# A transformer block in split fp32: engines chosen when the instruction list is made, other buffers for late norms and three X blocks, two x tiles by ScalarE's queue

## The chip, the cores and the metric

The kernel runs on one core of a Trainium2 chip. The metric is the time of one execution on the device in microseconds (us), the median of several runs. The core has five engines that run their own instruction lists beside each other: TensorE (PE; its weight loads are shown as PEld), VectorE (DVE), ScalarE (ACT), GpSimd (POOL) and SyncE (SP), which here issues nearly all DMAs. A matmul writes one of 8 PSUM banks of 128 x 512 fp32; only VectorE and ScalarE read them.

## The reference

One block: `h = x + A(layernorm(x))`, `h2 = h + B(layernorm(h))`, x of 2048 tokens by 448, all in fp32.

```python
def A(x):          # sliding-window attention, 16 heads of 28, window 256
    q, k, v = split(x @ wqkv)
    scores = q @ k.T * 28 ** -0.5, kept where 0 <= i - j < 256
    return (softmax(scores) @ v) @ wo
def B(x):          # gated GELU, 448 -> 1792 -> 448
    return (gelu_tanh(x @ w_gate) * (x @ w_up)) @ w_down
```

## The kernel before, in words

**Precision.** TensorE multiplies a rounded fp32 form (`F32R`). So each operand is split into a high part (`to_hi`, a copy on ScalarE) and a low part (`to_lo`, source minus high part, on VectorE or GpSimd), and a product is the sum of high x high, high x low and low x high.

**How the order is made.** Nothing is issued directly. Every operation is put on a list by `op(engine, cost, latency, key, fn, reads, writes, bank, port, ...)`; dependencies follow from the names that it reads and writes. `Lists.run` then plays the list through on the host with a simple clock: at each step each engine has candidates whose dependencies are met, and among those that could start within a few hundredths of a microsecond of the earliest the one with the lowest `key` is taken. The order that comes out is the order of the instructions on each engine; on the chip the engines only wait for each other. `port=True` marks operations of VectorE and GpSimd that the clock lets not overlap. `allowed` says which banks a kind of product may use, and `idle` fills TensorE's waits in the first microseconds with transposes of the identity. Most constants at the top of the file are keys or lags for this list.

**Start.** SP's queue loads the 16 x tiles (`load`, 128 tokens by 448 each, into `hres`), the q/k weights (`wqk_load`) and the v weights (`wv_load`). The first tiles are normalised (`layer_norms`, `normalise`), transposed on TensorE (`tr`, L454) and split into xT.

**Attention.** Four chunks of 512 tokens by four groups of four heads are 16 blocks. A block loads its q and k (`loads`, L711), makes scores (L729), maxima (L733), probabilities (L802, exponentials at L806), masks them on GpSimd (L821) and multiplies them with v (`attend`, L840); `MERGE` says whether a block's `attend` is one piece or two halves. `project_tile` (L678) makes q and k of the next chunk meanwhile, `values` (L624) v, `output` (L900) the product with wo.

**Feed-forward part.** 14 passes m, each for 256 columns of gate and up and 1024 tokens. The first three (`CL`) use plain products with 512 tokens a turn (`cslot`, `cfull`, L1139); the other 11 use one level of Strassen's scheme, 7 instead of 8 products of half-size blocks, two of them side by side in the array (`both`, L1340). For it the tokens are combined: `tokens_x(cp, ...)` loads blocks of the transposed normalised tokens (`loads_x`, L1010, and `fill`, L1016), makes sums (`XADD`, L1051 to L1057) and splits them (`split`, `XLO` for the low parts). Token half 0 puts all of its X blocks into `late[0]` (xo), which opens only when attention is over; half 1 puts them into xT, at the places in `XPLACE`. `weight_set` does the same with the weights: sums at L1210, low parts at L399 by `WLO` or `WLO2`, where a table names GpSimd or VectorE for each.

A product's bank is copied away by ScalarE (`copied`, L1346) or added to a buffer by VectorE (`added`, L1350), then Gelu (L1362, in the plain passes L1164), the product of gate and up (L1368, in the plain passes L1179) and the split into high and low part. The down product (`down_half`, L1414) uses half-height tiles, in two phases that write the same four banks with the halves exchanged; before the second phase a 1x1 read of the bank, `seen` (L1260, on ScalarE), makes TensorE wait until the first is complete. `out_add` (L1431) adds the finished banks to `hres` and stores them. All of TensorE's feed-forward operations are chained in one fixed order by `queued`; the down halves are put between the other products by `pause`.

The keys of the feed-forward part start at `FFN` = 1000 and grow by 2 x `UNIT` = 200 a pass. Norms of the feed-forward part (`ln2`) for tokens 0 to 1023 are made in attention, the rest in the first passes (`norms_later`); tiles from 8 on use three parts of the then free v buffer (`VM`). A tile goes out through `turn` (L490, L493) in transposed form.

Of the kernel before, what the change touches and what calls it, by code (L numbers as in the profile page):

```python
# [28 lines left out]
MERGE = (1, 1, 1, 0, 1, 1, 1, 1, 0, 1, 1, 1)  # L29
# [5 lines left out]
VLAST = (-22, 7, 26, 34)  # L35
ELAST = 1
LAG_P = 14.5
LAG_V = 11.0
EDGE = 12
WIN = 10  # L40
FFN = 1000
FULL = 3
CL = 3
CWL = 100
LATER = 4
ALONE = 5
# [7 lines left out]
WLO2 = ('pool', 'dve', 'pool', 'dve')  # L54
XADD2 = ('pool', 'pool', 'dve', 'dve')
XLO2 = ('pool', 'pool', 'dve', 'pool', 'dve')
XLATE = 150
XSTEP = 200
XWHOLE = (0, 0)
HASTE = 300  # L60
OUTK = 40
WLATE = 190
UNIT = 100
XADD = ('dve', 'dve', 'pool', 'dve')
XLO = ('dve', 'pool', 'dve', 'dve', 'dve')
WLO = ('dve', 'pool', 'dve', 'dve')
DKEY = 368
# [30 lines left out]
class Op:  # L98
    __slots__ = ("eng", "cost", "lat", "key", "fn", "deps", "users", "left", "banks", "port", "ready", "start", "fin",
                 "size", "tag", "mode")  # L100
# [9 lines left out]
class Lists:  # L110
# [6 lines left out]
    def op(self, eng, cost, lat, key, fn, r=(), w=(), bank=None, port=False, size=0, tag=None, after=(), part=None, mode=0):  # L117
        o = Op()
        o.eng, o.cost, o.lat, o.key, o.fn, o.port, o.size, o.tag, o.mode = eng, cost, lat, key, fn, port, size, tag, mode
        o.deps, o.users, o.ready, o.start = set(after), [], 0.0, None  # L120
        o.banks = () if bank is None else tuple(bank) if type(bank) is list else (bank,)
# [33 lines left out]
    def run(self, allowed, idle):  # L155
# [10 lines left out]
        for o in self.ops:  # L166
            o.left, o.ready, o.start = len(o.deps), 0.0, None
            for b in o.banks:
                b.k, b.left = None, 0
            if not o.left:  # L170
                cand[o.eng].append(o)
# [5 lines left out]
        def start_of(e, o):  # L177
            t = max(free[e], o.ready)
            if o.port:
                t = max(t, lock["pool" if e == "dve" else "dve"] - 0.03)  # L180
# [25 lines left out]
        while n:  # L206
            best = None
            for e in E:
                c = choice(e)
                if c is not None and (best is None or c[0] < best[0]):  # L210
                    best = c
            t, o, got = best
            e = o.eng
# [5 lines left out]
            cand[e].remove(o)  # L219
# [26 lines left out]
            for u in o.users:  # L246
                u.left -= 1
                u.ready = max(u.ready, o.start + cost if e == u.eng == "pe" else o.fin + WAKE[u.eng])
                if not u.left:
                    cand[u.eng].append(u)  # L250
# [4 lines left out]
def block_kernel(ctx: ExitStack, tc, x, wqk_in, wv_in, wo_in, gu_in, rest_in, cw_in, down_in, out):  # L255
# [122 lines left out]

    def HR(t):
# [60 lines left out]
    def normalise(t, key, kind):  # L440
# [3 lines left out]
        home = [VM[2 * t % 3], VM[(2 * t + 1) % 3]] if spare else [(lambda i=i: xn[i], XN(i), None) for i in range(2)]  # L444
# [36 lines left out]
        op("act", 0.49, 0.605, key, lambda: to_hi(xT[:, 0:4, c], view()), (), [XT(tc)], b)  # L481
        op("dve", 0.89, 0.87, key, lo, [XT(tc)], [XT(tc)], b)
# [13 lines left out]
    def turned(t, key, kind):  # L496
# [5 lines left out]
            put, [span("xT", tc, 0.5)])  # L502
        dma(key + 0.1, 80, lambda: nc.sync.dma_start(f(xT[:, 3, c]), d[D - 128:D]), put,
            [span("xT", tc + 0.5, 0.5)], cost=0.55)
# [16 lines left out]
    def start():  # L521
# [5 lines left out]
        for t in range(4):  # L527
            load(t, -100 + t)
        wv_load(0, -95)
# [23 lines left out]
        op("pool", 0.1, 0.1, -101, lambda: nc.gpsimd.memset(nhalf, -0.5), (), ["nhalf"])  # L553
# [63 lines left out]
    def values(t, p, n):  # L617
# [4 lines left out]
        for a in range(NP):  # L622
# [3 lines left out]
                stop=(a == NP - 1)), [XT(col(t)), *(WV(p + i, h, wb) for i in range(n))], () if a else [V(t, p, n)], b, tag="v")  # L626
# [40 lines left out]
    def project_tile(c, m):  # L667
# [7 lines left out]
        for a in range(NP):  # L675
# [4 lines left out]
                stop=(a == NP - 1)), [span("xT", cc, 4), WQK(m, h)], (), b, tag="proj")  # L680
# [18 lines left out]
    got = {}  # L699
# [232 lines left out]
    XPLACE = {(1, 0): (0, 0), (1, 2): (3, 0), (1, 1): (0, 1), (1, 3): (3, 1), (0, 0): (0, 2), (0, 1): (3, 2),  # L932
              (0, 2): (0, 3), (0, 3): (3, 3), (1, 4): (6, 0), (0, 4): (6, 1)}
# [5 lines left out]
    VM = [(lambda i=i: v_m[:, 512 * i:512 * i + 512], span("vm", 512 * i, 512), None) for i in range(7)]  # L939
# [851 lines left out]
```

## Time and profile before

| | |
|---|---|
| median of 3 runs | 698.39 us (696.53 to 698.69) |
| the profiled execution | 698.2 us, its span 696.5 us |
| mean granted TensorE clock | 0.999 |
| DMA | 116.25 MB, mean 167 GB/s |

The span goes from the first to the last instruction; the execution's own time holds 1.7 us more. In the lines of the profile, `L1340 PE MATMUL bank<-xT,proj` is a matmul issued by line 1340 of the file, which writes `bank` and reads `xT` and `proj`; `x12` counts instructions merged into one row; `[0.77 <-ACT e L1260]` is idle time of the engine ahead of it and what ended it.

### The profile page before, as it was taken

To read this page: it belongs to the slowest core of one execution; us is meant where nothing else is said; L and a number is where in the kernel's file an instruction comes from. 1 tells how busy PE (TensorE), PEld (TensorE's weight loads), DVE (VectorE), ACT (ScalarE), POOL (GpSimd) and SP (SyncE) were. 2 spreads that over 40 slices of the span, in tenths; PEclk is the share of its full clock that TensorE was granted. 3 is DMA by queue.
4 is the path that set the end of the run, shared out by engine and by line. 5 is a ranking of instruction groups with operands and counts; after the bars stand their busy time and mean duration, and the time that the engine had idled before them with its cause. 6 is when DMAs were issued, how large, how long until landed. Compare 5 with 4: busy or idle time off the path is not lost. (4 is left out here: it accounts for less than half of the span.)

```text
span 696.5 us, 15373 instructions
## 1 busy us (share of the span) xinstructions
PE 685.1 (98%) x5544; PEld 578.1 (83%) x5544; DVE 513.4 (74%) x1213; ACT 413.9 (59%) x911; POOL 311.1 (45%) x422
## 2 busy tenths in 40 slices
PE   8999999999999999999999999999999999999997
PEld 7888888888888878878878888888888888888886
DVE  7967678987798788838775789776555756866764
ACT  7747576877768667776554565644534545546431
POOL 5612654644456446441452779634303445447000
PEclk9999999999999999999999999999999999999999
DMA  9997967688688697406767775415004744533102
GB/s 315 277 285 216 286 173 202 183 230 244 166 210 247 183 273 207 165 1 178 197 181 158 213 205 170 119 51 171 20 16 131 211 132 132 161 116 88 44 15 105
DMA packets 104691, 116.25 MB, mean 167 GB/s; under 512 B 44632, under 2 KB 82392, under 8 KB 104040
## 3 DMA queue, kind: packets, MB, share of 16 engines
q1 hardware_dynamic: 104472, 115.17, 58.0%
q8 instruction: 43, 0.70, 0.4%
q14 instruction: 32, 0.26, 0.1%
q10 hardware_dynamic: 144, 0.11, 0.0%
HBM read 84.97 MB, written 44.47 MB: 186 GB/s over the span
## 5 line engine op out<-in xcount | busy, mean ns | idle before, releaser
L733 DVE CUSTOM_DVE_ANT_0 mt<-bank,mt 128x384 bf16<-128x384 f32 (+2 forms) x256 | 126.4, 526 | 26.8 <-PE bank L729 24.8
L806 ACT ACTIVATE pp<-bank 128x384 f32<-128x384 f32 (+1 forms) x188 | 90.8, 527 | 18.5 <-PE bank L802 16.3
L678 PE MATMUL bank<-xT 128*128 128x512 f32 x308 | 96.1, 399 | 0.0
L1340 PE MATMUL bank<-xT,proj 64*128 64x512 f32 x735 | 94.7, 389 | 0.2 <-DVE v L1350 0.2
L1340 PEld LDWEIGHTS bank<-xT,proj 64*128 64x128 f32 x735 | 72.1, 184 | 13.4 <-DVE v L1350 0.8
L729 PE MATMUL bank<-rk,rq 84*128 84x384 f32 (+2 forms) x256 | 81.0, 337 | 0.0
L802 PE MATMUL bank<-rq,rk 104*128 104x384 f32 (+2 forms) x352 | 80.6, 302 | 0.0
L821 POOL TENSOR_SCALAR_AFFINE_SELECT pp<-pp 128x512 f32<-128x512 f32 x96 | 60.6, 651 | 40.2 <-ACT pp L806 38.6
L1414 PE MATMUL bank<-proj,gh 64*128 64x448 f32 x624 | 71.5, 362 | 1.2 <-ACT e L1260 1.2
L802 PEld LDWEIGHTS bank<-rq,rk 104*128 104x128 f32 x352 | 59.4, 190 | 9.3 <-ACT pp L806 1.5
L1431 DVE TENSOR_TENSOR hres<-bank,hres 128x448 f32<-128x448 f32 (+1 forms) x113 | 62.8, 611 | 5.6 <-PE bank L1414 5.6
L1414 PEld LDWEIGHTS bank<-proj,gh 64*128 64x128 f32 x624 | 59.2, 184 | 8.0 <-ACT e L1260 1.9
L678 PEld LDWEIGHTS bank<-xT 128*128 128x128 f32 x308 | 55.6, 189 | 6.8 <-DVE proj L399 0.5
L1210 POOL TENSOR_TENSOR xn<-proj 64x128 f32<-64x128 f32 (+2 forms) x36 | 33.3, 928 | 52.5 <-DMA proj<-gu 46.8
L1260 ACT ACTIVATE e<-bank 1x1 f32<-1x1 f32 x139 | 21.7, 156 | 55.9 <-PE bank L1414 41.3
L729 PEld LDWEIGHTS bank<-rk,rq 84*128 84x128 f32 x256 | 47.6, 189 | 7.0 <-DVE mx L733 1.4
L396 ACT ACTIVATE rq<-bank 8x512 fp32r<-8x512 f32 x64 | 37.7, 589 | 22.1 <-PE bank L760 21.0
L399 DVE TENSOR_TENSOR proj<-proj 128x448 fp32r<-128x448 f32 (+2 forms) x42 | 25.8, 630 | 32.0 <-ACT proj L396 27.0
L624 PE MATMUL bank<-proj,xT 128*128 128x448 f32 (+1 forms) x220 | 49.1, 334 | 0.0
L1340 PE MATMUL bank<-xo,proj 64*128 64x512 f32 x366 | 47.7, 389 | 0.1
L1340 PEld LDWEIGHTS bank<-xo,proj 64*128 64x128 f32 x366 | 36.0, 184 | 7.1 <-DVE v L1350 0.8
L1350 DVE TENSOR_TENSOR raw<-bank,raw 128x512 f32<-128x512 f32 x22 | 15.2, 691 | 35.1 <-PE bank L1340 35.0
(193 smaller groups left out, 1474.3 us busy)
## 6 DMA issues: line engine op xcount, KB each, us to landing
rk<-k SPq DMA_DIRECT2D x44, 336.0 KB
rq<-q SPq DMA_DIRECT2D x32, 336.0 KB
gu<-in_gu_dram SPq DMA_DIRECT2D x18, 480.0 KB
proj<-gu SPq DMA_DIRECT2D x24, 288.0 KB
q<-proj SPq DMA_DIRECT2D x12, 448.0 KB
proj<-down SPq DMA_DIRECT2D x22, 224.0 KB
proj<-gu SPq DMA_DIRECT2D x24, 192.0 KB
k<-proj SPq DMA_DIRECT2D x9, 448.0 KB
```

The source lines that it names most:

```text
L396: nc.scalar.activation(dst, src, AF.Copy)
L624: op("pe", mm(224 * n), 0.29 if n == 1 else 0.38, key + a / 16, lambda a=a, h=h, wb=wb, xb=xb: nc.tensor.matmul(bank[b.k][:, 0:224 * n], x ...
L678: op("pe", mm(512) + 0.002, 0.403, key, lambda a=a, h=h, wb=wb, xb=xb: nc.tensor.matmul(bank[b.k], wqk[m][:, h, wb, :], xT[:, xb, cc * 128 ...
L729: nc.tensor.matmul(bank[b.k][:, o:384], rq[u][0:3 * DH, j, i * 128:i * 128 + 128], rk[u][0:3 * DH, j, m0 * 128:(i + 3) * 128], start=True, ...
L733: nc.vector.tensor_tensor_reduce(junk[s % 2][:, o:384], bank[b.k][:, o:384], mask[:, o:384], 1.0, -BIG, OP.add, OP.max, mx[:, i, j:j + 1])
L802: nc.tensor.matmul(bank[b.k][:, n * i:n * i + n], rk[u][0:104, j + i, m * 128:m * 128 + 128], rq[u][0:104, j + i, lo * 128:(hi + 1) * 128] ...
L806: nc.scalar.activation(pp_cols(o, n)[:, j:j + G], bank[b.k][:, 0:G * n].rearrange("p (g t) -> p g t", g=G), AF.Exp, scale=SCALE)
L821: nc.gpsimd.affine_select(a, a, pattern=[[0, 4], [-cm, 128]], compare_op=op_, fill=0.0, base=0, channel_multiplier=cm)
L1210: arith("pool", w, key + 1, lambda e: e.tensor_tensor(xn_m[HALF[side], o:o + w], a(), b(), op=what), rd, [tok])
L1340: nc.tensor.matmul(bank[b.k], w, xarea(u.cp, xl, xs, side)[:, xk], start=p in (1, 2, 5) and not k and not t, stop=t == 2, tile_position=(6 ...
L1414: nc.tensor.matmul(bank[banks[q].k][:, 0:D], h[oh][0]()[HALF[x], q * 128:q * 128 + 128], d[wh][0]()[HALF[x]], start=not ph and not y and n ...
L1431: op("dve", 0.07 + w * 0.463 / D, 0.163 + w * 0.463 / D, key, lambda: nc.vector.tensor_tensor(hres[:, t, c0:c0 + w], bank[b.k][:, c0:c0 + ...
```

## The change

- An operation may carry `alts`, for each engine that could do it the cost, the latency, the function and the port mark. It is a candidate on all of them; the one on which the list's clock would end it first gets it.
- With `FLEX = 'xwsc'` this holds for the X sums and low parts (x), the weight sums and low parts (w) (GpSimd or VectorE), `seen` (s) and `copied` (c) (ScalarE or VectorE). The tables `XADD`, `XLO`, `WLO` stay as first values only.
- X blocks (1,2), (1,1) and (1,0) of token half 0 lie in xT and are loaded from key `X0LOAD` on behind block 15's loads (`X0HOLD`); the other X blocks of both halves get other places.
- Late norms use two other parts of the v buffer and a part of `raw_m` (`SPARE`), and the plain passes' gate buffers move to `VM[0:4]`.
- x tiles 2 and 3 are issued by ScalarE, around a first small activation that brings the function table's loading there. `nhalf` is set ahead of it.
- Dependencies on xT are named by half (`XTB`): the four high parts and the three low parts apart.
- Keys and lags have other values. `MERGE` makes block 15's `attend` two halves instead of block 12's.

```diff
-MERGE = (1, 1, 1, 0, 1, 1, 1, 1, 0, 1, 1, 1)
+MERGE = (1, 1, 1, 0, 1, 1, 1, 1, 1, 1, 1, 0)
-VLAST = (-22, 7, 26, 34)
-ELAST = 1
+VLAST = (-10, 3, 26, 30)
+ELAST = 0
-LAG_V = 11.0
+LAG_V = 12.0
-WIN = 10
+WIN = 8
+FLEX = 'xwsc'
-CWL = 100
+CWL = 75
-CKEY = (220, 242)
-CWKEY = (236, 240, 190, 306)
-EARLY = (15, 16, 15, 15)
-CHOLD = (10, 13, 11, 13)
-X0KEY = 1060
-XTIME = (10, 6, 6)
-WFIRST = 1500
+CKEY = (220, 290)
+CWKEY = (226, 264, 238, 276)
+EARLY = (15, 15, 15, 15)
+CHOLD = (10, 12, 11, 13)
+X0KEY = 1200
+X0LOAD = 230
+X0HOLD = 15
+XTIME = (10, 6, 7)
+WFIRST = 1460
-XLATE = 150
+XLATE = 75
-HASTE = 300
+HASTE = 260
-WLATE = 190
+WLATE = 250
-DKEY = 368
+DKEY = 288
-HOLDD = (15, 13)
-EVICT = 150
+HOLDD = (15, 14)
+EVICT = 135
-LN1 = (-4, -14, 39, 120)
-LN2 = (146, 254)
-VKEY = (-39, -29, 40, 30)
+LN1 = (-8, -6, 35, 116)
+LN2 = (146, 260)
+VKEY = (-27, -38, 40, 18)
...
@@ Lists.op, Lists.run
+        if alts:
+            o.fn = lambda: alts[o.eng][2]()
...
+                for e in o.alts or (o.eng,):
+                    cand[e].append(o)
...
+                if o.alts and min(start_of(x, o)[0] + o.alts[x][1] for x in o.alts) < t + o.alts[e][1]:
+                    continue
...
+            if o.alts:
+                o.eng = e
+                o.cost, o.lat, _, o.port = o.alts[e]
...
@@ start
-        for t in range(4):
+        op("pool", 0.1, 0.1, -101, lambda: nc.gpsimd.memset(nhalf, -0.5), (), ["nhalf"])
+        for t in range(2):
             load(t, -100 + t)
+        op("act", 1.35, 1.45, -110, lambda: nc.scalar.activation(rcp[0][0:1, 0:1], nhalf[0:1, 0:1], AF.Copy), ["nhalf"], [("rcp", 0)])
+        for t in range(2, 4):
+            op("act", 0.44, 2.3 + 0.3 * (t - 2), -110 + t, lambda t=t: nc.scalar.dma_start(hres[:, t, :], xr[t * 128:(t + 1) * 128, :]),
+               (), [HR(t)])
...
-    XPLACE = {(1, 0): (0, 0), (1, 2): (3, 0), (1, 1): (0, 1), (1, 3): (3, 1), (0, 0): (0, 2), (0, 1): (3, 2),
-              (0, 2): (0, 3), (0, 3): (3, 3), (1, 4): (6, 0), (0, 4): (6, 1)}
+    XPLACE = [{(1, 2): (0, 3), (1, 1): (3, 3), (1, 0): (3, 2), (1, 3): 0, (0, 2): 3, (0, 1): 6, (0, 3): 9, (0, 0): 12,
+               (0, 4): 15, (1, 4): 16},
+              {(1, 2): 17, (1, 1): 20, (1, 0): 23, (1, 3): (0, 0), (0, 0): (3, 0), (0, 1): (0, 1), (0, 2): (3, 1),
+               (0, 3): (0, 2), (1, 4): (6, 0), (0, 4): (6, 1)}]
...
+    SPARE = [VM[5], VM[6], (lambda: raw_m[:, 1024:1536], span("raw", 1024, 512), None)]
-    cgbuf0, cubuf0, cgbuf = [*RAW, *EV], [VM[6], XNB], [*VM[3:7], EV[1]]
+    cgbuf0, cubuf0, cgbuf = [*RAW, *EV], [VM[6], XNB], [*VM[0:4], EV[1]]
...
@@ arith
+        ways = {"pool": (0.1 + n * 0.00225, 0.15 + n * 0.00225, lambda: fn(nc.gpsimd), port),
+                "dve": (0.07 + n * 0.00104, 0.17 + n * 0.00104, lambda: fn(nc.vector), port)}
...
@@ tokens_x, load
+            soon = not cp and type(XPLACE[cp][l, slot]) is tuple
+            dma(X0LOAD + 10 * k0 if soon else key, 131 * n, lambda: nc.sync.dma_start(
...
+                after=[got[X0HOLD]] if soon else chain[-1:])
...
@@ seen, copied
+        ways = {"act": (0.08, 0.17, lambda: nc.scalar.activation(e8[0:1, 0:1], bank[b.k][0:1, 0:1], AF.Copy), False),
+                "dve": (0.07, 0.17, lambda: nc.vector.tensor_copy(e8[0:1, 1:2], bank[b.k][0:1, 0:1]), False)}
+        op("act", 0.08, 0.17, key, ways["act"][2], (), (), b, alts=ways if "s" in FLEX else None)
...
+        ways = {"act": (0.49, 0.605, lambda: nc.scalar.activation(buf[0](), bank[b.k], AF.Copy), False),
+                "dve": (0.603, 0.7, lambda: nc.vector.tensor_copy(buf[0](), bank[b.k]), False)}
+        op("act", 0.49, 0.605, key, ways["act"][2], gate_of(buf), [buf[1]], b, alts=ways if "c" in FLEX else None)
```

More of the change, by code (lines that the diff above doesn't have):

```diff
@@ L209, in run @@
                 c = choice(e)
[L210 to L213, printed above, removed]
+                if c is not None and (best is None or c[0] < best[0][0]):
+                    best = c, e
+            t, o, got = best[0]
+            e = best[1]
             if e == "pe" and t > free["pe"] + 0.1:
@@ L377, in XT, with XTB @@
         return span("xT", t, 1)
+    def XTB(t, xb):
+        return span("xT", t, 1) if xb == 3 else span("xT", t + (xb > 3) / 2, 0.5)
     def HR(t):
@@ L443, in normalise @@
         spare = kind == "ln2" and t > 7
-        home = [VM[2 * t % 3], VM[(2 * t + 1) % 3]] if spare else [(lambda i=i: xn[i], XN(i), None) for i in range(2)]
+        home = [SPARE[2 * t % 3], SPARE[(2 * t + 1) % 3]] if spare else [(lambda i=i: xn[i], XN(i), None) for i in range(2)]
         x0, at0 = home[i2][0], home[i2][1]
@@ L679, in project_tile @@
                 bank[b.k], wqk[m][:, h, wb, :], xT[:, xb, cc * 128:cc * 128 + 512], start=(a == 0),
-                stop=(a == NP - 1)), [span("xT", cc, 4), WQK(m, h)], (), b, tag="proj")
+                stop=(a == NP - 1)), [*(XTB(cc + i, xb) for i in range(4)), WQK(m, h)], (), b, tag="proj")
         proj_ops[c, m] = L.ops[-NP:]
```

82 lines of the change are left out of this document (39 added, 43 removed).

## The prediction

> **What bounds the kernel now.** I read the page's head first, then the busy time by stretch, then TensorE's waits, then the chain that ended last, and last the order of time around the places where that chain leaves TensorE.
>
> ```profile
> span 696.5 us, 15373 instructions
> PE 685.1 (98%) x5544; PEld 578.1 (83%) x5544; DVE 513.4 (74%) x1213; ACT 413.9 (59%) x911; POOL 311.1 (45%) x422
> ```
>
> Busy time by stretch (columns: length; busy time and count of PE, PEld, DVE, ACT, POOL; granted clock, DMA share, GB/s), a start-up stretch, one of attention, the stage with the plain products of the feed-forward part, and the long stage of Strassen products:
>
> ```profile
> 9.00:30.00 21.00, 20.89 (x136) 18.01 (x134) 19.76 (x45) 17.39 (x33) 13.66 (x23) 1.00 0.94 314
> 150.00:200.00 50.00, 50.00 (x372) 41.42 (x371) 41.36 (x134) 33.20 (x68) 23.08 (x40) 1.00 0.78 214
> 322.00:376.00 54.00, 52.06 (x464) 42.88 (x464) 40.61 (x74) 30.60 (x77) 19.31 (x21) 1.00 0.74 187
> 400.00:674.00 274.00, 273.31 (x2482) 236.34 (x2480) 191.11 (x301) 138.92 (x344) 122.09 (x116) 1.00 0.39 113
> ```
>
> TensorE is busy everywhere at a granted clock of 1.00. The change adds and removes no matmul, so it can only win the places where TensorE stands still or starts late. In attention (50.00 of 50) there is nothing to win. The stage from 322 to 376 leaves 54 - 52.06 = 1.94 us. TensorE's waits name who made them:
>
> ```profile
> PE bank L1720 <- POOL ident L550: 2.1, 1, 2.1
> PE bank L1414 <- ACT e L1260: 1.9, 3, 0.8
> PE bank L1340 <- DVE v L1350: 0.5, 2, 0.4
> ```
>
> The second line is that stage: three waits for L1260, the 1x1 read by which ScalarE says that a bank may be written again. In order of time, one of the three, and behind it a pair of halves that ran without a wait:
>
> ```profile
> 345.00 2.61 PE L1414 MATMUL bank<-proj,gh 64*128 64x448 f32 x24
> ...
> 352.23 1.37 PE L1414 MATMUL bank<-proj,xT 64*128 64x448 f32 x12
> ...
> 353.18 0.68 DVE L399 TENSOR_TENSOR xo<-xo 128x512 fp32r<-128x512 f32 x1
> 353.22 1.06 ACT L1164 ACTIVATE v<-bank 128x512 f32<-128x512 f32 x2
> 354.18 0.34 ACT L1260 ACTIVATE e<-bank 1x1 f32<-1x1 f32 x2
> 354.37 1.50 PE L1414 MATMUL bank<-proj,xT 64*128 64x448 f32 x12 [0.77 <-ACT e L1260]
> ```
>
> The two bank reads stand behind two Gelus on ScalarE; undisturbed, the 24 matmuls take 2.61 us, here 352.23 to 355.87, that is 3.64.
>
> The last stage is read from the chain that ended last. Its passes (one m of the loop, marked by the 24 matmuls of the middle slot) have the same work, so the distance from mark to mark shows what each lost:
>
> ```profile
> 399.42 2.74 PE bank L1340 x24
> ...
> 427.03 2.74 PE bank L1340 x24
> ...
> 454.31 2.74 PE bank L1340 x24
> ...
> 481.22 2.74 PE bank L1340 x24
> ...
> 671.25 2.75 PE bank L1340 x24
> ```
>
> Ten passes take 671.25 - 399.42 = 271.83 us. The shortest shown (454.31 to 481.22) takes 26.91, the longest (399.42 to 427.03) 27.61. Ten of 26.91 would be 269.1, so 2.73 us are lost, at L1350, VectorE's add of a bank to a buffer, more than the 0.5 us of the waits tells, because each wait also costs the restart behind it.
>
> **The change part by part.** I sum against the profiled execution: 698.2 us, its span 696.5 plus 1.7 around it. The median of the runs shown is 698.39, so the two agree within 0.2.
>
> *Start-up, two x tiles by ScalarE's queue.*
>
> ```profile
> 0.79 1.81 SPq L525 DMA_DIRECT2D hres<-in_x_dram  x4
> ...
> 2.65 0.91 SPq L605 DMA_DIRECT2D pp<-in_wv_dram  x2
> ...
> 3.40 0.63 DVE L428 BATCH_NORM_STATS2 bnst<-hres 128x6 f32<-128x448 f32 x1 [1.42 <-DMA hres<-in_x_dram]
> ...
> 7.67 0.56 ACT L396 ACTIVATE proj<-pp 128x448 fp32r<-128x448 f32 x1
> ...
> 9.21 1.10 PE L624 MATMUL bank<-proj,xT 128*128 128x224 f32 x6
> ```
>
> Four issues take 1.81 us of SP's queue, so taking two out moves everything behind them, wv and wqk first, 0.9 us forward. That is the upper bound of the gain: real work starts on TensorE at 9.21, and the stretch from 9 to 30 is so full (20.89 of 21, DMA share 0.94) that an earlier start is partly paid back. ScalarE pays two issues of 0.45 (a quarter of 1.81) and a small first activation; in before it idles until its first normalisation at 5.65, so these hide, but the third tile's issue then stands behind the loading of the function table. The other end is that tile 0, whose landing at 3.40 starts everything, shares the engines with tile 2: two tiles of 224 KB at 314 GB/s take 1.5 us where one takes 0.7, so up to 0.7 later. I take -0.5, about half of the issue time, from -0.9 to +0.7. The Trainium skill, page DMA: Bandwidth & Descriptors, section Issuing engines are not separate DMA queues, says that a second issuing engine saves only sequencer time because all run on the same 16 engines; by that the term would lie near 0 wherever the engines are the limit, and the 0.94 agrees with it for all but the first microseconds.
>
> *Three X blocks loaded in attention.* Slots 2, 1 and 0 of the second operand half move into xT, which is free there; 3 x 6 = 18 of the 22 loads at L1010 can go behind block 15's loads.
>
> ```profile
> 275.91 0.43 SPq L711 DMA_DIRECT2D rk<-k  x1
> ...
> 323.42 4.31 SPq L1010 DMA_DIRECT2D xo<-xn  x7
> ```
> ```profile
> 300.00:310.00 10.00, 1.00 0.01 2
> ```
>
> Block 15's last load is issued at 275.91, and the DMA engines then fall to 0.01 at 300 to 310. At 4.31 / 7 = 0.62 us an issue, 18 cost 11 us of SP's queue there, beside nothing that TensorE waits for; the weight bounces and down loads queued behind them are wanted only after 322. So the move costs nothing and takes 18 x 131 KB = 2.4 MB out of the stage 322 to 376. It wins nothing by itself, since the first Strassen product at 376 finds X ready; it lets the X sums start when their buffers open instead of when the loads land.
>
> *Engines chosen when the list is made.* The bank read may go to VectorE, the PSUM copies too, the X and weight sums and low parts to GpSimd or VectorE, each where the list's clock ends it first.
>
> ```profile
> L1260 ACT ACTIVATE e<-bank 1x1 f32<-1x1 f32 x139 | 21.7, 156 | 55.9 <-PE bank L1414 41.3 <-PE bank L1340 7.8 <-PE bank L1139 4.4
> ...
> L1346 ACT ACTIVATE v<-bank 128x512 f32<-128x512 f32 x34 | 20.3, 599 | 27.1 <-PE bank L1340 24.9 <-DVE gh L399 1.7 <-PE bank L1139 0.5
> ```
> ```profile
> L1350 DVE TENSOR_TENSOR v<-bank,v 128x512 f32<-128x512 f32 x33 | 22.2, 687 | 8.5 <-PE bank L1340 8.3
> ...
> L1368 DVE TENSOR_TENSOR v<-raw,v 128x512 f32<-128x512 f32 x22 | 18.2, 827 | 0.0
> ...
> L1368 DVE TENSOR_TENSOR v<-e,v 128x512 f32<-128x512 f32 x11 | 11.1, 1006 | 0.0
> ...
> L1368 DVE TENSOR_TENSOR v<-bank,v 128x512 f32<-128x512 f32 x11 | 7.5, 680 | 0.0
> ```
> ```profile
> L399 POOL TENSOR_TENSOR xo<-raw,xo 128x512 fp32r<-128x512 f32 x3 | 3.9, 1287 | 0.0
> ```
>
> A read costs 0.156 on ScalarE; the trace has none on VectorE, so I bound it by 0.16 and by 0.69, a whole add. In the wait shown above VectorE is free at 353.86, so two reads there would end 0.3 before ScalarE's. If VectorE's sum of 353.18 is also gone to GpSimd (19.31 busy of 54), nothing is left of the wait. What can go in this stage is 1.94 idle plus 0.13 (1.50 against 1.37) at each of three restarts, 2.3 us. I take -1.4: one of the three whole, half of the others; from -2.3 to 0.
>
> In the Strassen passes 2.73 can go. VectorE has 191.11 busy of 274 and ScalarE 138.92, so copies have little reason to leave ScalarE (0.599 there, about 0.69 on VectorE by the nearest row), but weight sums that go to the freer of two engines shorten the queue in front of L1350. I take -1.3, half; the ends are -2.7 and a loss that the second rival prices.
>
> *New keys and lags in attention.* Only the order changes. TensorE has no gap to lose there, so this is 0 or worse; by the waits seen elsewhere, 0.4 to 0.8 each, I take one half-sized, +0.3, from 0 to +1.5. Late norms in other buffers, one pair of attend halves moved from block 12 to block 15: the same instructions, 0. The end of the kernel keeps its order, 0.
>
> Sum: -0.5 - 1.4 - 1.3 + 0.3 = -2.9, so 698.2 - 2.9 = 695.3 us. With every gain at its end, -0.9 - 2.3 - 2.7, it is 692.3.
>
> **The rivals.** *The waits only move.* The list chooses by its own clock; where VectorE and ScalarE are late together, as at 353.18 and 353.22, a read has nowhere better to go. Then 0.5 comes from the first stage, 0.6 from the passes, nothing at the start, +0.3 in attention: 697.4.
>
> *X comes too late.* X0KEY goes from 1060 to 1200, and the keys have 200 to a pass, so the sums may stand 140 / 200 x 26.91 = 18.8 us further back.
>
> ```profile
> 359.25 0.94 DVE L399 TENSOR_TENSOR xo<-e,xo 64x512 fp32r<-64x512 f32 x1
> ...
> 376.28 2.23 PE L1340 MATMUL bank<-xo,w 64*128 64x512 f32 x18
> ```
>
> The last one ends at 360.19, 16.1 us before it is read. If all of the shift came true, TensorE would wait 18.8 - 16.1 = 2.7 at 376, and the gains would be eaten: 698.0. Against it: keys only order what is ready at the same time, and the loads come earlier.
>
> *VectorE is jammed, slower.* Reads, copies and sums that go to VectorE stand in front of L1350, and sums that go to GpSimd hold VectorE up: the same 128x512 sum takes 0.680 with one operand in PSUM, but 0.827 and 1.006 in the mean with both in SBUF, beside GpSimd sums of 1.287. If every pass then lost what the worst one loses, 0.70, ten passes cost 7.0 instead of 2.73, +4.3; with -0.5, -1.4 and +0.3 that is 700.9. It turns the sum to zero from 0.43 a pass ((2.73 + 1.6) / 10; now 0.27) and is a loss beyond the bound from 0.64. For it: half the passes lose something already. Against it: the list prices the engines' queues, so it moves work to VectorE only where it finds it free. The Trainium skill, page SBUF — State Buffer, section Who interferes with whom, states that a VectorE instruction with two SBUF inputs and a GpSimd one that reads SBUF exclude each other for a whole instruction, and that one with a single SBUF input is untouched; by that rule each sum handed to GpSimd could hold VectorE up by its whole length. The 0.680 against 1.006 agrees.
>
> **How the numbers follow.** A difference counts here from 0.3% on, 2.1 us. The forecast has 0.60, the waits that only move 0.14, X too late 0.08, the jam 0.18. So faster 0.60, within the bound 0.22 (697.4 and 698.0), slower 0.18. The likeliest is 695.3. The range goes from the sum of all gains less 0.7 of scatter between runs (the three shown lie within 2.2), 691.6, to just short of the jam, 700.2. The forecast's own range is 692.3 to 696.3.
>
> **What would show it.** Right: L1260 appears on VectorE as well as ScalarE, TensorE's wait for it falls from 1.9 below 1; passes within 27.1 us, none of 27.6; 18 loads at L1010 between 276 and 310; first L624 at about 8.7. Wrong: L1350 or a new VectorE copy releasing TensorE in more passes than now, a gap at the first Strassen product, or gaps in attention, where there were none.

## The result, and the profile after

The changed kernel is slower, by 0.8%. Its median is 703.63 us (702.49 to 704.17, six runs) against 698.36 us (696.16 to 699.25, six runs), a ratio of 1.0081 [1.0063, 1.0099]. The forecast was 695.3, its range ended at 700.2. The profiled execution of the changed kernel took 702.49 us, the lowest of its six; its granted clock was 1.00 in the mean, that of the other five 0.996 to 0.998.

First the head of the page of the changed kernel:

```profile
span 700.7 us, 15231 instructions
PE 688.6 (98%) x5536; PEld 600.1 (86%) x5536; DVE 558.1 (80%) x1386; ACT 401.5 (57%) x835; POOL 202.5 (29%) x326
```

VectorE has 45 us more work than before (513.4), GpSimd 109 us less (311.1), ScalarE 12 us less. Where it stands is in the busy time by stretch (length; busy time and count of PE, PEld, DVE, ACT, POOL; clock, DMA share, GB/s), changed kernel:

```profile
322.00:376.00 54.00, 53.24 (x472) 44.68 (x472) 46.19 (x90) 28.57 (x66) 11.59 (x16) 1.00 0.66 162
400.00:450.00 50.00, 47.75 (x423) 43.08 (x421) 48.65 (x91) 29.23 (x64) 14.08 (x14) 1.00 0.53 156
400.00:674.00 274.00, 271.26 (x2446) 250.79 (x2444) 221.00 (x424) 132.00 (x292) 34.45 (x38) 1.00 0.39 114
```

The same stretch 400 to 450 in the kernel before:

```profile
400.00:450.00 50.00, 49.85 (x450) 42.49 (x448) 44.69 (x62) 31.68 (x77) 37.95 (x33) 1.00 0.57 164
```

The plain-product stage (322 to 376) did improve: TensorE stands still for 0.76 us instead of 1.94. But in 400 to 450 TensorE lost 2.25 us instead of 0.15, while VectorE was busy for 48.65 of 50 and GpSimd for 14.08 instead of 37.95. The chain of waits of the changed kernel, marked as before by the 24 matmuls of each pass's middle slot (now L1369):

```profile
399.94 2.74 PE bank L1369 x24
...
430.36 2.90 PE bank L1369 x23
...
458.48 2.74 PE bank L1369 x24
...
485.35 2.74 PE bank L1369 x24
...
675.70 2.75 PE bank L1369 x24
```

The first mark is only 0.52 late. The next two passes take 30.42 and 28.12 us (before 27.61 and 27.28), the third 26.87, like the best pass before. Ten passes take 275.76 instead of 271.83, 3.93 us more, of which 3.65 lie in the first two.

The page counts a wait as short, but the restart behind it costs too. So I also made a sum of lost time from the start times of TensorE's matmuls in the trace: the time, less what all earlier matmuls need when each takes the usual interval of its kind. By stretch, in us:

| stretch | before | after | difference |
|---|---|---|---|
| up to 60 | 7.81 | 8.99 | +1.18 |
| 60 to 322 (attention) | 1.71 | 1.26 | -0.45 |
| 322 to 376 (plain products) | 2.06 | 1.30 | -0.76 |
| 376 to 400 | 0.25 | 0.77 | +0.52 |
| 400 to 460 (two passes) | 1.73 | 5.37 | +3.64 |
| 460 to 675 | 4.13 | 4.32 | +0.19 |

Together +4.32, and the profiled executions differ by 702.49 - 698.2 = 4.29. The medians differ by 5.3, because the other five runs of the changed kernel took 0.8 to 1.7 longer than the profiled one.

TensorE's waits in the changed kernel, and the order of time around the longest one in the passes:

```profile
PE bank L1751 <- POOL ident L573: 2.1, 1, 2.1
PE bank L1369 <- DVE e L1289: 1.5, 1, 1.5
PE bank L472 <- ACT xn L467: 1.3, 1, 1.3
PE bank L1445 <- DVE xT L417: 0.7, 1, 0.7
PE bank L1445 <- DVE e L1289: 0.6, 2, 0.3
```
```profile
410.76 1.49 POOL L417 TENSOR_TENSOR xo<-v,xT 128x512 fp32r<-128x512 f32 x1 [3.83 <-ACT xT L414]
...
411.12 1.54 DVE L1237 TENSOR_TENSOR xn<-proj 64x384 f32<-64x384 f32 x1
...
412.69 0.69 DVE L417 TENSOR_TENSOR xo<-e,xT 128x512 fp32r<-128x512 f32 x1
...
413.30 0.69 DVE L417 TENSOR_TENSOR xo<-xo,xT 128x512 fp32r<-128x512 f32 x1
...
413.90 1.28 DVE L1381 TENSOR_TENSOR v<-bank,v 128x512 f32<-128x512 f32 x2
...
415.10 0.14 DVE L1289 COPY e<-bank 1x1 f32<-1x1 f32 x1
...
415.24 0.73 PE L1369 MATMUL bank<-xo,proj 64*128 64x512 f32 x3 [1.53 <-DVE e L1289]
```

This is a queue on VectorE: a weight sum (L1237), two low parts of X (L417), then the adds that empty the banks (L1381, in the kernel before L1350), then the 1x1 read. TensorE waits for the last. The weight sum takes 1.54 us there, beside a GpSimd operation of 1.49; the groups give the means, changed kernel first, then the kernel before:

```profile
L1288 ACT ACTIVATE e<-bank 1x1 f32<-1x1 f32 x72 | 11.5, 159 | 57.9 <-PE bank L1445 42.2 <-PE bank L1369 7.6 <-PE bank L1166 6.7
...
L1289 DVE COPY e<-bank 1x1 f32<-1x1 f32 x67 | 9.7, 144 | 15.0 <-PE bank L1445 13.7 <-PE bank L1166 0.3
...
L1399 DVE TENSOR_TENSOR v<-e,v 128x512 f32<-128x512 f32 x11 | 7.7, 700 | 0.0
...
L1237 DVE TENSOR_TENSOR xn<-proj 64x384 f32<-64x384 f32 x12 | 7.6, 637 | 0.4
...
L1237 DVE TENSOR_TENSOR xn<-proj,xn 128x384 f32<-128x384 f32 x12 | 6.6, 552 | 0.4
```
```profile
L1210 POOL TENSOR_TENSOR xn<-proj,xn 128x384 f32<-128x384 f32 x12 | 13.2, 1098 | 14.1 <-DVE w L399 5.6 <-DVE proj L399 4.7 <-ACT v L1346 3.5
```

The sum of 1.54 is one of the twelve whose mean is 0.64 with it. A weight sum costs 0.55 us on VectorE and 1.10 on GpSimd. The list's own prices (`ways` in the change, n = 384) have the same sense, 0.57 against 1.01 to the end of the operation, so it chooses VectorE unless VectorE could start more than 0.44 later. In this row all 12 sums went there.

### The profile page after: what moved, and what is told of

The parts are those of the page before. It is cut to its first block, busy times and chain, and to the rows that moved or that the text cites. A ratio compares the mean times of both kernels' runs of the same rounds, so it can differ in the third digit from the quotient of the medians.

```text
span 700.7 us, 15231 instructions
## 1 busy us (share of the span) xinstructions
PE 688.6 (98%) x5536; PEld 600.1 (86%) x5536; DVE 558.1 (80%) x1386; ACT 401.5 (57%) x835; POOL 202.5 (29%) x326
## 4 chain that ended last, share of the span: by engine, by line
PE 87%; DVE 6%; DMA 3%; issue 1%; ACT 1%; SPq 1%; POOL 0%; DVEq 0%
PE bank L1369 23%; PE bank L1445 16%; PE bank L700 10%; PE bank L824 7%; PE bank L751 6%; PE bank L862 6%; PE bank L646 5%; PE bank L1166 5%; PE bank L922 5%; PE bank L1178 2%; DVE hres L1462 2%; DMA proj<-gu 1%; PE bank L472 1%; DVE proj L417 1%; DMA hres<-in_x_dram 1%
## 5 line engine op out<-in xcount | busy, mean ns | idle before, releaser
L1369 PE MATMUL bank<-xT,proj 64*128 64x512 f32 x645 | 122.3, 388 | 0.0
L1369 PE MATMUL bank<-xo,proj 64*128 64x512 f32 x456 | 100.0, 389 | 1.5 <-DVE e L1289 1.5
L1369 PEld LDWEIGHTS bank<-xT,proj 64*128 64x128 f32 x645 | 84.6, 184 | 5.6
L1445 PE MATMUL bank<-proj,gh 64*128 64x448 f32 x624 | 75.9, 363 | 0.0
L1445 PEld LDWEIGHTS bank<-proj,gh 64*128 64x128 f32 x624 | 65.3, 184 | 3.8 <-DVE hres L1462 0.3
L1369 PEld LDWEIGHTS bank<-xo,proj 64*128 64x128 f32 x456 | 63.7, 184 | 5.1 <-DVE e L1289 1.9
L1369 PE MATMUL bank<-xT,w 64*128 64x512 f32 x276 | 54.8, 389 | 0.0
L646 PE MATMUL bank<-proj,xT 128*128 128x448 f32 (+1 forms) x220 | 52.8, 337 | 0.0
L414 ACT ACTIVATE rq<-bank 8x512 fp32r<-8x512 f32 x64 | 37.6, 588 | 25.2 <-PE bank L782 24.2
L1369 PE MATMUL bank<-xo,w 64*128 64x512 f32 x240 | 50.7, 390 | 0.1
L1288 ACT ACTIVATE e<-bank 1x1 f32<-1x1 f32 x72 | 11.5, 159 | 57.9 <-PE bank L1445 42.2
L1445 PE MATMUL bank<-proj,xT 64*128 64x448 f32 x312 | 41.3, 371 | 1.7 <-DVE xT L417 0.7
```

The lines of the kernel that those rows point to most:

```text
L414: nc.scalar.activation(dst, src, AF.Copy)
L646: op("pe", mm(224 * n), 0.29 if n == 1 else 0.38, key + a / 16, lambda a=a, h=h, wb=wb, xb=xb: nc.tensor.matmul(bank[b.k][:, 0:224 * n], x ...
L1369: nc.tensor.matmul(bank[b.k], w, xarea(u.cp, xl, xs, side)[:, xk], start=p in (1, 2, 5) and not k and not t, stop=t == 2, tile_position=(6 ...
L1445: nc.tensor.matmul(bank[banks[q].k][:, 0:D], h[oh][0]()[HALF[x], q * 128:q * 128 + 128], d[wh][0]()[HALF[x]], start=not ph and not y and n ...
```

## The experiments

Each stands against the kernel before on the same chip (medians 697.78 to 698.17). Those of the first and second group make the list anew, so that more than the named part can move.

**The changed kernel with one part undone.** Theory: weight sums on VectorE jam it. Rivals: the keys of the second X half, the start, all free choice.

*Weight sums and their low parts fixed again.*

```diff
-FLEX = 'xwsc'
+FLEX = 'xsc'
```


> The changed kernel with FLEX 'xsc': the weight sums stay on GpSimd and their low parts on VectorE, all else as changed. Theory 1 (the weight sums that the list hands to VectorE jam it from 400 to 456 us, 48.65 of 50 busy, and cost the 4 us lost there): GpSimd's busy time in 400 to 674 goes back from 34 towards 100 us, VectorE's in 400 to 450 falls below 45, the loss there falls from 4 to about 1, and the time to about 700.5. Theory 2 (the X sums of the second token half, asked for earlier, make the jam): 703 to 704 as before. Theory 3 (the start alone is the loss, the rest is noise of a new order): 703 to 704.

700.84 us, ratio 1.0044 [1.0029, 1.0059]: 2.8 us come back. Busy time of the stretch 400 to 450 in this kernel:

```profile
400.00:450.00 50.00, 49.19 (x435) 40.89 (x433) 43.60 (x82) 28.12 (x64) 31.81 (x24) 1.00 0.56 163
```

VectorE falls by 5.05 us, GpSimd rises by 17.73, and TensorE's standstill falls from 2.25 to 0.81. In the lost time, 376 to 675 falls from 10.46 to 9.02, while the plain stage loses 0.6 more; the profiled executions differ by only 1.1 (702.49 and 701.38), and the rest of the 2.8 lies between runs that were not profiled. Two things stay: the stages from 376 on still lose 2.9 more than in the kernel before (9.02 against 0.25 + 1.73 + 4.13 = 6.11), though VectorE is no busier there from 400 to 450 than it was (43.60 against 44.69); and over 400 to 674 VectorE keeps 205.98 us of work, about half of what it had gained (191.11 before, 221.00 changed), from the other free operations.

*Keys of the second X half as before.*

```diff
-XTIME = (10, 6, 7)
+XTIME = (10, 6, 6)
...
-XLATE = 75
+XLATE = 150
```


> The changed kernel with XTIME and XLATE of the kernel before (the X blocks of the second token half asked for later, weight sums still free). Theory 1: the weight sums still crowd VectorE, 702 to 704. Theory 2: the jam from 400 to 456 is spread, about 700.5. Theory 3: no change, 703.6.

704.44 us, 1.0098 [1.008, 1.0116]. Nothing comes back. But the keys hardly moved the load: VectorE is busy for 29.52 of the 30 us from 400 to 430, and 29.71 in the changed kernel. So the run does not clear the X sums.

*All x tiles by SP's queue, without the small activation.*

```diff
-        for t in range(2):
+        for t in range(4):
             load(t, -100 + t)
-        op("act", 1.35, 1.45, -110, lambda: nc.scalar.activation(...
-        for t in range(2, 4):
-            op("act", ...
```


> The changed kernel with all x tiles issued by SP's queue and without the small first activation. Theories 1 and 2: the 1.1 us that the start loses (first normalisation input at 4.49 instead of 3.40) come back, and part of it is eaten in attention: 702.6 to 703.1. Theory 3: the whole loss comes from here and the order that follows, below 700.

711.39 us, 1.0191 [1.017, 1.0211]. The first statistics are back at 3.36 and the lost time at 15 us is 8.45, less than before. But the list came out otherwise in attention: lost time grows to 18.6 at 322. The price was not in the start, so the run says only that the start itself can be had back. What it showed of the clock stands at the end.

*No free choice.* `FLEX = ''` with all the new keys.

> The changed kernel with FLEX empty: every engine as the tables name it, reads and copies on ScalarE. Theory 1: the jam goes as in no_w, but the stage from 322 to 376 loses the 0.75 us that the free reads won there: 701 to 702. Theory 2: 703.5 to 705. Theory 3: 703.6.

705.48 us, 1.0106 [1.0087, 1.0125]. The longest wait of TensorE, 5.5 us, starts at 421. The down product (L1445) waits for a low part of the gated product, in a buffer that lies in xT. That low part stands on VectorE behind another one, which takes 4.12 us while GpSimd runs its own operations without a pause:

```profile
421.17 1.26 POOL L417 TENSOR_TENSOR xo<-v,xT 128x512 fp32r<-128x512 f32 x1
421.23 4.12 DVE L417 TENSOR_TENSOR proj<-proj 128x448 fp32r<-128x448 f32 x1
422.39 1.25 POOL L417 TENSOR_TENSOR xT<-xT 64x512 fp32r<-64x512 f32 x1
423.61 1.25 POOL L417 TENSOR_TENSOR xT<-v,xT 128x512 fp32r<-128x512 f32 x1
...
425.27 1.48 DVE L417 TENSOR_TENSOR xT<-v,xT 128x512 fp32r<-128x512 f32 x1
...
426.80 1.49 PE L1445 MATMUL bank<-proj,xT 64*128 64x448 f32 x6 [5.51 <-DVE xT L417]
```

A low part of that form (`proj<-proj`, 128x448) takes 0.64 in the mean in the changed kernel. Here it is GpSimd's work that holds VectorE up, and not VectorE's own. Undoing the whole choice tells nothing of its parts.

**The kernel before with one part added.** The edit adds the choice (`alts`) to the kernel before and frees only what is named.

*Weight sums and low parts:* `FLEX = 'w'`.

> The kernel before, with its own keys, and only the weight sums and low parts free to go to VectorE or GpSimd when the list is made. Theory 1 (the free weight sums crowd VectorE): GpSimd's busy time from 400 to 674 falls from 122 to below 50, VectorE's rises from 191 to about 215, 2 to 3 us are lost between 376 and 460, time about 700.5. Rival (the crowd comes from the new keys, the free choice itself is harmless): 697.5 to 698.5.

705.29 us, 1.0103 [1.0088, 1.0118]. Lost time at 376 is 11.55 as before, at 460 already 18.3 (before 13.6): the loss appears in the passes, without any other part of the change. It is 7.4 us in all, where 700.5 us was expected, and the order was made anew here.

*Reads and copies:* `FLEX = 'sc'`.

> The kernel before with only the bank reads and copies free to go to VectorE. If the 0.75 us that the changed kernel wins between 322 and 376 come from the free reads: 697.0 to 697.8, TensorE's wait for the read below 1.2 us. If copies on VectorE stand in front of the adds: over 699.

702.30 us, 1.0065 [1.0049, 1.008]. Two effects of opposite sign: lost time at 376 is 1.5 less than before (10.07), and 2.3 more at 675 (19.97). The profiled execution, at 700.82, is the shortest of five, so the 2.3 is less than the median's 4.4. The choice helps in the plain products and harms in the Strassen passes, where a bank copy on ScalarE (1.5 us) leads TensorE's waits.

*Only the start,* and, in the changed kernel, *only the place of the two issues* (`after=[table]`, behind the small activation):

> The kernel before with only the start changed: x tiles 2 and 3 by ScalarE's queue around the small first activation. If the start by itself costs: the loss at 15 us goes from 8.65 to about 9.8 and the time to 699 to 700. If a changed start also upsets the order that the list makes behind it: gaps in attention beyond that, over 701. If attention takes the loss back: 698.4.

> The changed kernel, but ScalarE issues x tiles 2 and 3 behind its first activation, so that tile 0 has the DMA engines to itself. If the start's 1.1 us come from tile 2 sharing with tile 0: the first statistics at about 3.4 instead of 4.49, the loss at 15 us back from 9.8 to about 8.6, and 702.5 if the order behind it holds (an order that does not hold would show as new gaps in attention). If they come from ScalarE's own work at the start: no earlier statistics, 703.6.

714.30 us (1.0231 [1.0216, 1.0246]) and 710.47 us (1.0178 [1.0163, 1.0193]). The loss came in attention in both: lost time at 322 is 21.98 and 19.65. The list made anew from a shifted start loses 9 to 12 us more there than the kernel that it was made from, so parts cannot be priced in this way. TensorE's granted clock has a part in it: it was 0.83 from 250 to 260 and 0.79 from 310 to 326 in the first kernel, and 0.83 from 270 to 290 in the second. The first statistics start at 4.01 and 3.90. The second kernel does not test what it was made for: its two issues go out at 0.97 and 1.38, while the function table loads and before the small activation runs at 2.08, so tile 0 was never alone on its way.

**The order held fixed.** These kernels make the list exactly as the kernel before (or the changed one) does, with the same engines and costs, and then issue one kind of operation on another engine. Every other instruction keeps its place.

*The kernel before, x tiles 2 and 3 issued by ScalarE:*

```diff
-            dma(key, 224, lambda: nc.sync.dma_start(hres[:, t, :], ...
+            by = nc.scalar if t in (2, 3) else nc.sync
+            dma(key, 224, lambda: by.dma_start(hres[:, t, :], ...
```


> The list of the kernel before, unchanged, but x tiles 2 and 3 are emitted on ScalarE's queue. Theory A: first statistics later by 0.5 to 1.1, loss at 15 us above 9, time 698.5 to 699.5. Theory C (a start that differs from the one the list was made for upsets attention on the chip itself, not only the list): gaps in attention, over 701.

698.99 us against 697.78, 1.0014 [1.0005, 1.0022]: the two issues alone, without the small activation, cost 1.2 us. The first statistics start at 4.34 instead of 3.40, and in its profile TensorE ran a stretch at half clock (before 1.00, and 18 matmuls in it):

```profile
10.00:12.00 2.00, 2.00 (x11) 2.00 (x10) 1.91 (x5) 2.00 (x5) 1.93 (x2) 0.50 1.06 380
```

*The kernel before, all weight sums issued on VectorE:*

```diff
-            arith("pool", w, key + 1, lambda e: e.tensor_tensor(xn_m[HALF[side], ...), rd, [tok])
+            arith("pool", w, key + 1, lambda e: e.tensor_tensor(xn_m[HALF[side], ...), rd, [tok], put="dve")
... (and in `arith`: `put`, where given, names the engine that issues)
```


> The list of the kernel before, unchanged, but all weight sums are emitted on VectorE instead of GpSimd, at the same places. Theory 1 (the sums jam VectorE where it has X sums as well): VectorE's busy time from 400 to 450 rises from 44.7 to 48 or more, 2 to 4 us are lost there, time 700.5 to 702.5. Rival (the sums fit between the other work, VectorE takes half of GpSimd's time for each and is freed from its blocking): 697.5 to 698.5.

701.23 us against 697.78, 1.0049 [1.0036, 1.0062]: +3.45 us from this alone. Its stretch of passes:

```profile
400.00:674.00 274.00, 272.43 (x2456) 240.35 (x2454) 212.54 (x370) 137.95 (x343) 53.82 (x44) 1.00 0.39 113
```

VectorE goes from 191.11 to 212.54. The loss is not in the same two passes: lost time grows by 6.2 from 460 to 675 (before 4.1) and by 2.6 from 400 to 460 (before 1.7). TensorE also stands still for 0.87 us from 376 to 400, where it had no gap before, and for less in the plain stage (1.07 instead of 1.94).

*The same for the first weight set only* (`put="dve" if n == 0`):

> The list of the kernel before, unchanged, but the five sums of the first weight set alone are emitted on VectorE (in r_wdve the loss at 380 was 0.7 below the kernel before, and turned at 390). If the place decides, that is VectorE's load at that moment: the 0.7 stays to the end, 697.0 to 697.4. If not: 697.8.

698.16 us against 698.08, 1.0002 [0.9989, 1.0015]: five sums in one place cost nothing that can be measured.

*The changed kernel, all reads and copies issued on ScalarE:*

```diff
-                "dve": (0.07, 0.17, lambda: nc.vector.tensor_copy(e8[0:1, 1:2], ...), False)}
+                "dve": (0.07, 0.17, lambda: nc.scalar.activation(e8[0:1, 0:1], ...), False)}
... (and the same for the copies)
```


> The changed kernel's list, unchanged, but bank reads and copies are all emitted on ScalarE, at the same places. If reads on VectorE are what gave 0.75 us back between 322 and 376: that is lost again, 704 to 705. If reads queued behind a crowded VectorE hold TensorE at 413 (there it waited 1.5 us for such a read): that wait goes, 702 to 703.

703.90 us, 1.008 [1.0066, 1.0094], no change. The wait shown above stays, and now names what stood in front of the read:

```profile
PE bank L1369 <- DVE v L1381: 1.4, 1, 1.4
```

So the read on VectorE was the messenger; the late thing was the add, behind the sums. The plain stage keeps its gain, too:

```profile
322.00:376.00 54.00, 53.14 (x466) 43.53 (x466) 45.55 (x79) 30.00 (x76) 11.12 (x16) 1.00 0.65 160
```

TensorE stands still for 0.86 us, 0.76 with the reads on VectorE and 1.94 before.

*The changed kernel, weight sums and low parts issued by the tables of before* (sums on GpSimd):

> The changed kernel's list, unchanged, but weight sums and low parts are emitted on the engines that the tables of the kernel before name (sums on GpSimd). If the sums on VectorE alone make the jam: VectorE's busy time from 400 to 450 falls from 48.65 to about 44, the waits at 413 and 421 (1.7 and 0.9) go, 700.5 to 701.5. If the order that the list made around fast sums is what binds (ScalarE's splits standing where a sum on GpSimd, 1.1 instead of 0.55, is not done yet): new waits behind ScalarE, 703 to 705.

710.30 us, 1.0181 [1.0165, 1.0197], outside both expectations. VectorE falls to 43.82 of 50 in 400 to 450, but TensorE now waits for reads, copies and low parts in places where it never did. An order made for sums of 0.55 us does not fit sums of 1.1, so this is no price of the sums.

*The changed kernel, x tiles 1 to 3 issued together on SP:*

> The changed kernel's list is made exactly as in the changed kernel, and only at emission the x tiles 1, 2 and 3 go out together on SP's queue; every engine keeps its order otherwise. Theory A (sharing the DMA engines makes tile 0 land late, and everything after just follows): first statistics at about 3.4 instead of 4.49, loss at 15 us back from 9.8 to about 8.7, time 702.4 to 703.0, no new gaps in attention. Theory B (the start is absorbed by attention anyway): 703.6.

703.67 us, 1.008 [1.0067, 1.0093]. Statistics start at 3.38, but the v weights, behind three tiles now, and tile 2 come later, and lost time at 10 us is 9.06 as in the changed kernel. Its profile also has half the clock from 12 to 14 us. It is no clean undoing, and it decides nothing of the cause; an early first tile alone did not bring the time back here.

**A version from what was found.** The kernel before, with free choice for reads and copies in the plain passes alone:

```diff
-        op("act", 0.08, 0.17, key, ..., alts=ways if "s" in FLEX else None)
+        op("act", 0.08, 0.17, key, ..., alts=ways if "s" in FLEX and key < FFN + 2 * UNIT * CL - EVICT else None)
... (and the same for the copies)
```


> The kernel before, reads and copies free between ScalarE and VectorE only in the plain passes (in b_sc the loss at 380 was 1.5 below the kernel before, and 4 were lost from 390 to 460). If the free choice in the Strassen passes lost them: 696.3 to 697.0. If the new order behind the plain passes lost them, since the keys were set for another: above 699.

697.15 us against 698.08, 0.9988 [0.9978, 0.9998], faster than both kernels by a little. The stage in it:

```profile
322.00:376.00 54.00, 53.19 (x474) 43.91 (x475) 44.43 (x89) 29.48 (x65) 19.36 (x21) 1.00 0.75 190
```
TensorE's three waits for a read, on VectorE now, cost 0.8 instead of 1.9, and lost time at 376 is 10.24 instead of 11.58.

## Why the prediction was wrong

**The Strassen passes, -1.3 forecast: the step that failed.** The text said that "weight sums that go to the freer of two engines shorten the queue in front of L1350". The runs show the contrary. The list does not take the freer engine but the one that would end the operation first, and at 0.55 against 1.10 us that is mostly VectorE, even when GpSimd is idle: GpSimd fell from 122.09 to 34.45 of 274 us, VectorE rose from 191.11 to 221.00. In place of -1.3 the trace has +3.93 in its ten passes, and +4.35 from 376 on. Moving only the sums, in the order of before, costs 3.45. Taking sums and low parts back in the changed kernel, with its order made anew, gives 2.8 by the medians, but in the profiled executions only 1.44 of the 4.35. So that weight sums on VectorE cost time, instead of winning it, is shown; that they are the whole loss of the passes is not. That the cost gathers in the passes from 400 to 458, because the X sums of the second token half are there too, fits VectorE's 48.65 of 50 and the queue shown, but no run separates it; with the order of before the loss spread over later passes.

**The jam rival was the right one,** and its price for the passes came out by luck: it said that every pass would lose 0.70, ten of them 7.0, and by the same reckoning they lost 275.76 - 269.1 = 6.7. But the first lost 3.5, the second 1.2 and the other eight 0.24 each in the mean. It missed the time (700.9) because the start and the plain stage were taken over from the forecast. Its chance of 0.18 was too low for a bad reason: "the list prices the engines' queues, so it moves work to VectorE only where it finds it free". A step-by-step choice prices the operation in hand; it does not see the add that becomes ready a moment later and then stands behind it. Half of its mechanism did not act here. GpSimd does hold VectorE up when both read SBUF: the 1.54 at 411.12 is an instance, the 4.12 in the kernel without free choice a larger one, and the same product of two buffers (now L1399) fell from 1006 to 700 ns as GpSimd emptied. The Trainium skill, page SBUF — State Buffer, section Who interferes with whom, says that a VectorE instruction with two SBUF inputs contends with a GpSimd one that reads SBUF, and these figures agree. But the change emptied GpSimd, so this went the good way in the mean, and the jam came from VectorE's own added work.

**The start, -0.5 forecast (-0.9 to +0.7): wrong in sign, and outside its bounds.** The issues alone cost 1.2. They moved as said: the v weights go out at 1.69 instead of 2.65. ScalarE's second issue did not wait behind the loading of the function table, as the text had it; it goes out at 1.29. The start of the changed kernel:

```profile
0.79 0.41 ACTq L550 DMA_DIRECT2D hres<-in_x_dram  x1
...
1.69 0.91 SPq L627 DMA_DIRECT2D pp<-in_wv_dram  x2
...
4.49 0.63 DVE L446 BATCH_NORM_STATS2 bnst<-hres 128x6 f32<-128x448 f32 x1 [2.51 <-DMA hres<-in_x_dram]
...
7.55 1.12 PE L472 MATMUL bank<-ident,xn 128*128 128x128 f32 x4 [1.32 <-ACT xn L467]
...
9.84 0.50 PEld L646 LDWEIGHTS bank<-proj,xT 128*128 128x128 f32 x2 [0.23 <-ACT xT L414]
```

Tile 0 lands 1.09 later (4.49 against 3.40), with tile 2 under way from the same moment. So it is throughout: the first statistics start at 4.01 to 4.49 in the eight traces in which ScalarE issues the two tiles at 0.79 and 1.29, and at 3.34 to 3.49 in the seven in which SP issues all four one after the other. I had bounded this by 0.7, from a rate of 314 GB/s and two tiles, while the weights too had been pulled forward into the same moments. TensorE is slower there as well. The first transposing products of the kernel before:

```profile
6.47 0.66 PE L454 MATMUL bank<-ident,xn 128*128 128x128 f32 x4 [0.65 <-ACT xn L449]
```

Four of them take 0.66 before and 1.12 after. In the changed kernel such products start every 0.21 us up to 11.2 and every 0.11 from then on; in the kernel before it is 0.11 from 5.3 on. The clock column does not show this, because the trace's first clock record is at 11.3 (before, at 5.2). How much of the 1.2 is the late tile and how much this clock, no run separates. And the first product of v (L646) starts at 9.84, released by the transposed x tile, not by the weights that had been brought forward: I shortened the path that did not end last. The rule of the Trainium skill that I set beside this (page DMA: Bandwidth & Descriptors, section Issuing engines are not separate DMA queues) was nearer with its 0, though the start came out worse than 0.

**The plain-product stage, -1.4 forecast: right in direction, too large, the cause only in part.** L1260 appears on both engines (72 and 67) at 0.144 on VectorE, and one wait for it is left in the stage, 0.28 instead of 1.9:

```profile
353.96 1.64 PE L1445 MATMUL bank<-proj,xT 64*128 64x448 f32 x12 [0.28 <-DVE e L1289]
```

The sign that the text named, a wait below 1, holds for this stage alone; with the passes TensorE waits 1.5 + 0.6 = 2.1 for the reads. The stage's lost time falls by 0.76, and the kernel before with this choice in the plain passes alone reaches -1.3 by 376. So the choice makes the gain. That it does so because VectorE makes the read is not borne out: with all reads issued on ScalarE in the same order the gain stayed (0.86 us of standstill). Why only half of it is left in the changed kernel is open. Nothing points at the weight sums: with them fixed on GpSimd the stage lost 0.6 more, not less.

**X blocks in attention, 0 forecast: right.** 18 loads behind block 15's, in 14.46 us of SP's queue instead of the 11 reckoned, and the first Strassen product without a gap in front of it, so the rival of the late X has no support either:

```profile
277.36 14.46 SPq L1036 DMA_DIRECT2D xT<-xn  x18
```
```profile
376.21 0.43 PE L1369 MATMUL bank<-xo,w 64*128 64x512 f32 x2
```

**New keys in attention, +0.3 forecast (0 to +1.5):** -0.45 by the table, just past the end of its range. **The end, 0:** right, 25.0 us from the last mark to the end of the span, before 25.2. The rival in which waits only move was no case: one stage gained and another lost.

**Left open.** The sums (3.45) and the start (1.2) make 4.7 of the 5.3, but they were measured in the order of before, and in the changed kernel the sums give back 2.8. From 376 on 2.9 us stay without the free weight sums. No run splits how much of that is the copies in the passes, which lost time in the order of before but gave nothing back in that of after, the X sums and low parts, whose free choice was never tried or undone alone, and the new keys. Nor is it settled how much of the difference between the profiled run and the others is the clock in the first 20 us.

## What to carry to other kernels

An order built step by step that lets each operation take the engine that ends it first fills the faster engine, and the operation that another engine waits for comes too late in an in-order queue: look which engine empties the contended buffers, and keep optional work off it. The other engine is no free place either, where its work holds the first one up (4.12 us instead of 0.64). Give the choice only where the profile shows a wait that it can end; here the plain stage alone gained. To price a part of a change in a kernel whose order is computed, hold the order fixed and move only that part, since an order made anew moved the time by up to 16 us, mostly for causes of its own. Start from the order of before: taking the sums out of the order that was made for them cost 6.7 us more (710.30 against 703.63).

## What was unexpected of the hardware

A short standstill of TensorE was followed by microseconds at half clock. In the kernel with all x tiles on SP's queue (busy time by stretch, columns as above):

```profile
150.00:152.00 2.00, 1.64 (x29) 0.72 (x21) 0.79 (x2) 0.81 (x2) 0.00 (x0) 1.00 1.10 237
152.00:154.00 2.00, 1.21 (x7) 0.88 (x7) 1.19 (x5) 1.94 (x4) 1.10 (x2) 1.00 1.08 276
154.00:156.00 2.00, 2.00 (x9) 1.70 (x9) 1.94 (x7) 1.69 (x4) 0.79 (x2) 0.67 0.72 166
156.00:158.00 2.00, 2.00 (x7) 1.48 (x7) 1.28 (x6) 1.96 (x6) 1.31 (x2) 0.50 0.68 160
```

TensorE idled for 1.15 us within four microseconds, in pieces of at most 0.7, and then had 0.50 to 0.67 of its clock until about 161. The Trainium skill, page TensorE: Matmul & The Clock Gate, section Part 1: The HAM clock gate (the "warmup" mystery), states that the clock halves after an idle window of about 3.4 us; here a partly idle stretch was enough. A larger single gap elsewhere had no such effect (the 1.53 at 415 in the changed kernel), so the size of one gap alone does not decide it.

The start shows it more often. Of the nine traces in which ScalarE issues x tiles 2 and 3, eight have TensorE at half clock in a stretch that ends between 10.8 and 14.1 us; in some it has not yet come to the full clock, in others it falls back for 3.4 us. In the seven in which SP issues all of them, from a list made so, it is at full clock from 7.9 us at the latest and does not fall back in the start. The late first tile and the late clock go together there; that the one brings the other is not shown.
